# Scores and second mixing as four 64x64 array tiles instead of two 64x128 tiles

## The chip, the cores and the metric

The kernel runs on one core of one Trainium2 chip. The metric is the device time of one execution in microseconds. The time before is the median of nine runs. A profile is one further execution, recorded by the hardware profiler; its durations belong to that execution.

## The reference

Talking-heads attention over 8 batches, 12 heads, 448 positions and a head dimension of 64, followed by a feed-forward network with a squared ReLU:

```python
scores = scale * np.matmul(q, k.transpose(0, 1, 3, 2))        # scale = 1/8
scores = np.einsum('bhij,hg->bgij', scores, w_pre)            # first mixing of heads
attn = np.exp(scores - np.max(scores, axis=-1, keepdims=True))
attn = attn / (np.sum(attn, axis=-1, keepdims=True) + 1e-09)
attn = np.einsum('bhij,hg->bgij', attn, w_post)               # second mixing of heads
out = np.matmul(attn, v)                                      # to x: 3584 x 768
h = np.maximum(x @ w_in, 0.0)                                 # w_in: 768 x 2048
y = (h * h) @ w_out                                           # w_out: 2048 x 768
```

## The kernel before

The work of a batch goes through these stages, each with its line in the profile:

- **Transposes** (`turn_unit`, L162): q and k arrive with positions on the partitions; TensorE turns them, two heads at a time, into `qT` and `kT` with the head dimension on 64 partitions per head. Each matmul uses 112 rows and 64 columns of the array.
- **Scores** (`score_pair`, L295): for one pair of heads and one block of 128 query positions, each head is one matmul. Its 64 contraction rows are the lower or the upper half of the partitions, its stationary side is 128 query positions wide, and its moving side is the 448 key positions. ScalarE copies one head's result to the tile `S`, VectorE the other's (L298). A batch has four blocks, and a block six pairs of heads: 192 pairs in all.
- **Gather** (`gather`, L310): a DMA on SP's queue re-lays ten query positions of all twelve heads, 120 rows by 448, from `S` to `G`.
- **First mixing** (`mix`, L317): one matmul with the stationary `pre` mixes the heads. ScalarE takes the exponential and the row sum (L321), VectorE the reciprocal (L323), and GpSimd (POOL in the profile) scales the row and subtracts 1/448 into one of the tiles `d` (L325). The rows of `d` stand in two groups of 60, at partitions 0 and 64.
- **Second mixing** (`unmix`, L346): it takes two such tiles of `d` at a time. For each tile, each of four residues `r` of the key position and each row group `y`, a matmul has 60 rows and 128 key positions of `d` as the stationary side and 60 columns of `post` as the moving one, so a block has 2 x 4 x 2 = 16 matmuls. The results of `y = 0` and `y = 1` go to two PSUM banks, and VectorE copies each into `at` (L353). There are 180 blocks.
- **Attention times v** (`av_unit`, L181): 112 rows and 64 columns of the array, with ScalarE adding a bias on the way out (L192).
- **The FFN** (`ffn1_unit`, L228, and `ffn2_unit`, L258): full 128x128 matmuls (the last rows of a batch 128x64), with ReLU on ScalarE (L236), the square on GpSimd (L237) and VectorE's copy to the output (L265).

TensorE and GpSimd run in the order in which the program issues their instructions; the other engines are ordered by a scheduler. A loop over steps `ds` mixes two tiles of ten query positions, issues `unmix` for the two of two steps earlier (`LAG = 2`), puts score pairs and gathers ahead by ten tiles (`AHEAD`), and fills the space in between with FFN units of the batch before, by a budget in nanoseconds written into the program. All PSUM banks, eight of them, come from one pool, `psp`.

A matmul in the program becomes two instructions: a weight load of the stationary side (PEld in the profile) and the matmul proper (PE). The tile of the array that it uses follows from its row count, its column count and the partitions at which its operands and its result start.

Of the kernel before, what the change touches and what calls it, by code (L numbers as in the profile page):

```python
# [14 lines left out]
B, H, S, D = 8, 12, 448, 64  # L15
# [5 lines left out]
PR = S // R  # L21
# [4 lines left out]
BLK_START = [0, 120, 240, 320]  # L26
# [3 lines left out]
HR = H * HQ  # L30
# [13 lines left out]
def kernel(  # L44
# [11 lines left out]
    nc = tc.nc  # L56
    P = nc.NUM_PARTITIONS
# [9 lines left out]
    def bank(name, dtype=F32):  # L67
        return psp.tile([P, 512 if dtype == F32 else 1024], dtype, name=name, tag="ps")
# [44 lines left out]
    post = consts.tile([P, H, HQ], BF16, name="post")  # L113
# [4 lines left out]
    post = post[:, :, :].rearrange("p g i -> p (g i)")  # L118
# [19 lines left out]
    qTs, kTs, bvecs, xts, h2ts, ats = {}, {}, {}, {}, {}, {}  # L138
# [149 lines left out]
    def score_pair(b, blk, p):  # L288

        if (b, blk) not in Sb:  # L290
            Sb[(b, blk)] = work.tile([P, H, S], BF16, name="S", tag="S", bufs=2)
        pss = [bank("s_ps") for _ in range(2)]
        for hh in range(2):
            rs = slice(64 * hh, 64 * hh + 64)
            nc.tensor.matmul(pss[hh][:, 0:S], lhsT=qTs[b][rs, p, BLK_START[blk]:BLK_START[blk] + P],  # L295
                             rhs=kTs[b][rs, p, :], start=True, stop=True)
        for hh, copy in enumerate((nc.scalar.copy, nc.vector.tensor_copy)):
            copy(out=Sb[(b, blk)][:, 2 * p + hh, :], in_=pss[hh][:, 0:S])  # L298

# [29 lines left out]
    def place_of(s):  # L329
        b, t = s  # L330
        part = sum(t >= x for x in PARTS[b % 2]) - 1
        if (b, part) not in ats:
            ats[(b, part)] = attn[(3 * b + part) % 2]
        return ats[(b, part)], 2 + IQ * (t - PARTS[b % 2][part])

    def unmix(pair):

        places = [place_of(s) for s in pair]
        us = [bank("at_ps") for _ in range(2)]
        for x, s in enumerate(pair):  # L340
            d = dsb.pop(s)
            for r in range(R):
                for y in range(2):
                    rows = slice(64 * y, 64 * y + HR)
                    c = 4 * HR * x + HR * r
                    nc.tensor.matmul(us[y][:, c:c + HR], lhsT=d[rows, PR * r:PR * r + P], rhs=post[rows, :],  # L346
                                     start=True, stop=True)
        (at, c), (at2, c2) = places
        for y in range(2):
            src = us[y][0:PR, 0:8 * HR].rearrange("p (x m i) -> p m x i", x=2, i=HQ)  # L350
            if at is at2:
                dst = at[0:PR, :, :, c:c + 2 * IQ].rearrange("p r g (x z i) -> p (r g) x z i", z=2, i=HQ)
                nc.vector.tensor_copy(out=dst[:, :, :, y, :], in_=src)  # L353
            else:
                for x, (a, p) in enumerate(places):
                    dst = a[0:PR, :, :, p + HQ * y:p + HQ * y + HQ].rearrange("p r g i -> p (r g) i")
                    nc.vector.tensor_copy(out=dst, in_=src[:, :, x, :])
# [20 lines left out]
    with tc.manual_schedule(engines={PE, POOL}):  # L378
        for x in range(4):
            if x < 3:  # L380
                turn_unit(0, 1, x)
                turn_unit(0, 0, x, nc.scalar.copy)
            if x > 0:
                score_pair(0, 0, 2 * x - 2)
                score_pair(0, 0, 2 * x - 1)
# [26 lines left out]
        def scores_for(ds):  # L412
            tile = 2 * ds + AHEAD + 2
            blk = sum(tile >= x for x in starts) - 1
            if blk + 1 >= len(blocks):
                return
            if blk == 3:
                want = NPAIR * 4 + 2 * max(0, ds - FIRST_TURN[1])
            else:
                into, size = tile - starts[blk] - 2, starts[blk + 1] - starts[blk] - 2  # L420
                want = NPAIR * (blk + 1) + -(-NPAIR * into // size)
            while issued[0] < min(want, NPAIR * (blk + 2)):
                score_pair(*blocks[issued[0] // NPAIR], issued[0] % NPAIR)
                issued[0] += 1
# [12 lines left out]
        for ds in range(nd + LAG):  # L437
# [23 lines left out]
            if old2:  # L461
                unmix(old2)
                for b1, t1 in old2:
                    ends = PARTS[b1 % 2]
                    if t1 + 1 in ends:
                        part = ends.index(t1 + 1) - 1
                        for u in av_units(b1, part):
                            at_step(ds + 1, u)
                        if b1 == 0:
                            c = (IQ * ends[part], min(IQ * ends[part + 1], S))  # L470
                            at_step(ds + 1, (0, lambda c=c: filler.extend(ffn1_units(0, *c))))
                    if t1 == NT - 1:
                        if b1 > 0:
                            at_step(ds + 1, (0, lambda b1=b1: filler.extend(ffn1_units(b1))))
                        at_step(ds + 1, (0, lambda b1=b1: filler.extend(ffn2_units(b1))))
# [38 lines left out]
```

The softmax here doesn't subtract the row's maximum and nothing guards it: scores larger than these inputs give would overflow.

## Time and profile before

| | |
|---|---|
| median of 9 runs | 629.05 us (626.99 to 630.07) |
| profiled execution | 629.31 us, span of its trace 627.5 us |
| TensorE matmuls (PE) | busy 575.4 us, 7,530 instructions |
| TensorE weight loads (PEld) | busy 321.5 us, 7,530 instructions |
| VectorE / ScalarE / GpSimd | busy 423.0 / 396.4 / 409.3 us |
| granted TensorE clock, mean | 0.975 |

The span runs from the first to the last instruction of the trace. Matmuls are pipelined and their ends are modelled, so a matmul's duration is a latency; what it costs is the distance from its start to the next start. A group's row reads: line, engine, operation, output<-input, shapes, count, then busy time and mean duration, then the idle time before it and what ended it. In the TensorE rows "60\*128 60x60" means 60 rows and 128 columns of the array, and a moving operand of 60 partitions by 60 elements.

### The profile page before, as it was taken

The numbers are of one execution on the slowest core, as the hardware profiler recorded it, in microseconds if no ns is written. First come the engines' busy times: TensorE is split into PE (matmuls) and PEld (weight loads), VectorE is DVE, ScalarE is ACT, GpSimd is POOL, SyncE is SP. The second block draws the span as 40 slices with busy tenths as digits, with TensorE's granted clock in tenths as the row PEclk, the third lists the DMA queues.
The fourth block names the chain that finished last, engine by engine and source line by source line (L and its number), as shares of the span: only waits on it lengthen the run. The fifth ranks groups of instructions, "written<-read, shape, count | busy, mean of one in ns | idle before, by whom it ended". The sixth has DMA issues, their size and how long they took to land.

```text
span 627.5 us, 19617 instructions
## 1 busy us (share of the span) xinstructions
PE 575.4 (92%) x7530; PEld 321.5 (51%) x7530; DVE 423.0 (67%) x1082; ACT 396.4 (63%) x1196; POOL 409.3 (65%) x615
## 2 busy tenths in 40 slices
PE   4466898899999999999999999999999999999897
PEld 3123565655545555545645455545545555555554
DVE  3365886888777677866877677767877777654101
ACT  3455676677677757776677647876678657862320
POOL 6374959876388835895388835896387646872450
PEclk9965999999999999999999999999999999999899
DMA  9999969779547965587546964587553755422002
GB/s 139 191 193 186 178 122 151 131 105 171 135 90 115 159 138 106 97 130 112 121 104 112 156 137 101 97 134 120 119 102 75 129 121 102 76 58 76 15 11 78
DMA packets 90882, 73.64 MB, mean 117 GB/s; under 512 B 6308, under 2 KB 87716, under 8 KB 90788
## 3 DMA queue, kind: packets, MB, share of 16 engines
q1 hardware_dynamic: 51842, 49.57, 35.1%
q0 software_dynamic: 38816, 22.81, 28.4%
q8 instruction: 59, 0.97, 0.6%
q14 instruction: 35, 0.29, 0.1%
q10 hardware_dynamic: 130, 0.01, 0.0%
HBM read 45.63 MB, written 11.01 MB: 90 GB/s over the span
## 4 chain that ended last, share of the span: by engine, by line
PE 63%; POOL 10%; DMA 9%; ACT 7%; DVE 5%; issue 2%; SPq 2%; ACTq 0%; DVEq 0%; POOLq 0%
PE o_ps L258 22%; PE h_ps L228 19%; DMA G<-S 8%; PE m_ps L317 8%; PE at_ps L346 6%; POOL d L325 4%; PE s_ps L295 4%; PE ot_ps L181 4%; POOL h L237 3%; ACT xt L192 3%; ACT e_sb L321 3%; PE tr_ps L162 2%; DVE at L353 2%; SPq L310 2%; DVE S L298 1%
## 5 line engine op out<-in xcount | busy, mean ns | idle before, releaser
L325 POOL TENSOR_SCALAR d<-e_sb,rc 128x448 bf16<-128x448 f32 x360 | 225.6, 638 | 164.6 <-DVE rc L323 162.2
L321 ACT ACTIVATE e_sb<-m_ps 128x448 f32<-128x448 f32 x360 | 195.1, 556 | 77.2 <-PE m_ps L317 64.3
L353 DVE CAST at<-at_ps 112x480 bf16<-112x480 f32 x352 | 221.5, 669 | 32.8 <-PE at_ps L346 31.8
L228 PE MATMUL h_ps<-xt,w 128*128 128x448 bf16 (+2 forms) x960 | 168.2, 316 | 2.8 <-ACT e_sb L321 1.4
L258 PE MATMUL o_ps<-w,h 128*128 128x384 bf16 (+1 forms) x1024 | 162.5, 327 | 1.3 <-POOL h L237 1.3
L237 POOL TENSOR_TENSOR h<-hr 128x448 bf16<-128x448 f32 (+2 forms) x160 | 123.7, 780 | 28.8 <-ACT hr L236 26.0
L228 PEld LDWEIGHTS <-w 128*128 128x128 bf16 x960 | 82.6, 98 | 78.0 <-issue 21.0
L258 PEld LDWEIGHTS <-h 128*128 128x128 bf16 (+1 forms) x1024 | 85.3, 100 | 70.0 <-issue 15.5
L298 ACT CAST S<-s_ps 128x448 bf16<-128x448 f32 x192 | 99.8, 549 | 29.9 <-PE s_ps L295 20.1
L298 DVE CAST S<-s_ps 128x448 bf16<-128x448 f32 x192 | 112.5, 607 | 6.3 <-PE s_ps L295 3.2
L317 PE MATMUL m_ps<-G,pre 120*128 120x448 bf16 x360 | 104.9, 366 | 12.9 <-DMA G<-S 9.7
L323 DVE RECIPROCAL rc<-sm 128x1 f32<-128x1 f32 x360 | 54.6, 158 | 92.0 <-ACT e_sb L321 89.7
L236 ACT ACTIVATE hr<-h_ps 128x448 f32<-128x448 f32 (+2 forms) x136 | 68.3, 502 | 46.8 <-PE h_ps L228 31.1
L295 PE MATMUL s_ps<-kT,qT 64*128 64x448 bf16 x384 | 74.2, 373 | 13.6 <-ACT S L298 8.5
L346 PEld LDWEIGHTS <-d 60*128 60x128 bf16 x2880 | 53.7, 94 | 63.7 <-issue 46.9
L346 PE MATMUL at_ps<-post,d 60*128 60x60 bf16 x2880 | 75.0, 190 | 5.1 <-ACT xt L192 1.3
L321 ACT ACTIVATION_READ_ACCUMULATOR e_sb<-m_ps 128x1 f32 x360 | 77.8, 216 | 0.0
L192 ACT ACTIVATE xt<-ot_ps,bvec 128x160 bf16<-128x160 f32 (+3 forms) x144 | 42.5, 391 | 44.9 <-PE ot_ps L181 31.4
L317 PEld LDWEIGHTS <-pre 120*128 120x128 bf16 x360 | 29.2, 98 | 53.2 <-issue 20.9
L265 DVE COPY osb<-o_ps 128x384 f32<-128x384 f32 x48 | 26.5, 553 | 40.0 <-PE o_ps L258 39.1
L181 PE MATMUL ot_ps<-at,v 112*64 112x160 bf16 (+4 forms) x1152 | 44.7, 237 | 3.5 <-DVE at L353 3.5
L181 PEld LDWEIGHTS <-v 112*64 112x64 bf16 x1152 | 41.1, 114 | 7.4 <-issue 6.5
(36 smaller groups left out, 193.5 us busy)
## 6 DMA issues: line engine op xcount, KB each, us to landing
G<-S SPq DMA_DIRECT2D x352, 105.0 KB
kst<-in_k_dram POOLq DMA_DIRECT2D x24, 224.0 KB, 5.9
qst<-in_q_dram POOLq DMA_DIRECT2D x24, 224.0 KB, 5.7
v<-in_v_dram POOLq DMA_DIRECT2D x24, 224.0 KB, 6.6
w<-in_moe_w_in_dram POOLq DMA_DIRECT2D x8, 384.0 KB, 10.5
w<-in_moe_w_out_dram POOLq DMA_DIRECT2D x8, 384.0 KB, 7.7
out_dram<-osb SPq DMA_DIRECT2D x8, 336.0 KB
out_dram<-osb SPq DMA_DIRECT2D x8, 288.0 KB
```

The lines of the kernel that those rows point to most:

```text
L181: nc.tensor.matmul(ps[64 * hh:64 * hh + 64, TW * y + c0:TW * y + 2 + n], lhsT=vs[b][0:PR, g, r, :], rhs=at[0:PR, r, g, c0:2 + n], start=(y ...
L228: nc.tensor.matmul(ps[:, 0:n], lhsT=w1[ft // 4][:, c2, ft % 4 * 128:ft % 4 * 128 + 128], rhs=xts[b][:, c2, c0:c1], start=(c2 == 0), stop=( ...
L236: nc.scalar.activation(out=hr[:, 0:n], in_=ps[:, 0:n], func=ACT.Relu)
L237: nc.gpsimd.tensor_tensor(out=h2ts[(b, ft)][:, c0:c1], in0=hr[:, 0:n], in1=hr[:, 0:n], op=ALU.mult)
L258: nc.tensor.matmul(dst, lhsT=h2ts[(b, ft)][:, mt * 128:mt * 128 + ROWS[mt]], rhs=w2[ft // 4][:, ft % 4, n2 * 384:(n2 + 1) * 384], start=(f ...
L295: nc.tensor.matmul(pss[hh][:, 0:S], lhsT=qTs[b][rs, p, BLK_START[blk]:BLK_START[blk] + P], rhs=kTs[b][rs, p, :], start=True, stop=True)
L298: copy(out=Sb[(b, blk)][:, 2 * p + hh, :], in_=pss[hh][:, 0:S])
L317: nc.tensor.matmul(ps[:, 0:S], lhsT=pre[0:n, :], rhs=Gs.pop(s)[0:n, :], start=True, stop=True)
L321: nc.scalar.activation(out=e[:, :], in_=ps[:, 0:S], func=ACT.Exp, scale=SCALE, accum_out=sm[:, 0:1])
L325: nc.gpsimd.tensor_scalar(out=d[:, 0:S], in0=e[:, :], scalar1=rc[:, 0:1], scalar2=-1.0 / S, op0=ALU.mult, op1=ALU.add)
L346: nc.tensor.matmul(us[y][:, c:c + HR], lhsT=d[rows, PR * r:PR * r + P], rhs=post[rows, :], start=True, stop=True)
L353: nc.vector.tensor_copy(out=dst[:, :, :, y, :], in_=src)
```

## The change

Each score matmul is split into two with 64 query positions each, written to the lower and the upper 64 partitions of the same bank. Each matmul of the second mixing is split the same way, over its 128 key positions. Both therefore use tiles of 64 rows by 64 columns: a pair of heads takes four matmuls instead of two, a block of the second mixing 32 instead of 16. The moving operands (448 and 60 columns), the results in PSUM, the copies and the order of the stages stay as they were. In the second mixing the four tiles of a residue `r` follow one another: `y = 0` lower and upper half, then `y = 1`; in the scores likewise with the head `hh`.

```diff
@@ score_pair
         for hh in range(2):
             rs = slice(64 * hh, 64 * hh + 64)
-            nc.tensor.matmul(pss[hh][:, 0:S], lhsT=qTs[b][rs, p, BLK_START[blk]:BLK_START[blk] + P],
-                             rhs=kTs[b][rs, p, :], start=True, stop=True)
+            for z in (0, 64):
+                q0 = BLK_START[blk] + z
+                nc.tensor.matmul(pss[hh][z:z + 64, 0:S], lhsT=qTs[b][rs, p, q0:q0 + 64],
+                                 rhs=kTs[b][rs, p, :], start=True, stop=True)
@@ unmix
                     rows = slice(64 * y, 64 * y + HR)
                     c = 4 * HR * x + HR * r
-                    nc.tensor.matmul(us[y][:, c:c + HR], lhsT=d[rows, PR * r:PR * r + P], rhs=post[rows, :],
-                                     start=True, stop=True)
+                    for z in (0, 64):
+                        nc.tensor.matmul(us[y][z:z + 64, c:c + HR], lhsT=d[rows, PR * r + z:PR * r + z + 64],
+                                         rhs=post[rows, :], start=True, stop=True)
```

## The prediction

> **What bounds the kernel now.** I read the page's busy table and slices first, then the stage windows, then the groups, then the timeline of TensorE in a settled stretch.
>
> ```profile
> span 627.5 us, 19617 instructions
> PE 575.4 (92%) x7530; PEld 321.5 (51%) x7530; DVE 423.0 (67%) x1082; ACT 396.4 (63%) x1196; POOL 409.3 (65%) x615
> PEclk9965999999999999999999999999999999999899
> DMA  9999969779547965587546964587553755422002
> PE 63%; POOL 10%; DMA 9%; ACT 7%; DVE 5%; issue 2%; SPq 2%; ACTq 0%; DVEq 0%; POOLq 0%
> ```
>
> TensorE is busy for 92% of the span and holds 63% of the chain that ended last; DMA is full only in the first slices. The windows by stage (columns: length, busy time of each engine, clock, DMA share) separate the two:
>
> ```profile
> 30.00:80.00 50.00, 36.63 (x518) 19.89 (x513) 34.27 (x94) 29.72 (x93) 36.36 (x60) 0.74 1.06 185
> 80.00:580.00 500.00, 484.39 (x6571) 271.25 (x6569) 371.14 (x939) 344.31 (x1057) 344.28 (x515) 1.00 0.63 115
> ```
>
> Before 80 us the DMA queues are full and TensorE waits for them at a low clock. From 80 to 580 us TensorE is busy 97% at full clock and no other engine passes 75%. In that stretch nearly every nanosecond added to TensorE's stream is added to the time. The two groups that the change edits are:
>
> ```profile
> L295 PE MATMUL s_ps<-kT,qT 64*128 64x448 bf16 x384 | 74.2, 373 | 13.6 <-ACT S L298 8.5
> L346 PEld LDWEIGHTS <-d 60*128 60x128 bf16 x2880 | 53.7, 94 | 63.7 <-issue 46.9
> L346 PE MATMUL at_ps<-post,d 60*128 60x60 bf16 x2880 | 75.0, 190 | 5.1 <-ACT xt L192 1.3
> ```
>
> "64\*128" and "60\*128" say that both already run as tiles of 64 rows by 128 columns, two at a time. The 190 ns is a latency and not a cost. The cost is read from the timeline of TensorE (start, length, line, count):
>
> ```profile
> 302.11 0.55 PE L317 MATMUL m_ps<-G,pre 120*128 120x448 bf16 x2
> 302.49 1.46 PE L258 MATMUL o_ps<-w,h 128*128 128x384 bf16 x8
> 303.88 0.39 PE L346 MATMUL at_ps<-post,d 60*128 60x60 bf16 x16
> 304.12 0.35 PE L295 MATMUL s_ps<-kT,qT 64*128 64x448 bf16 x2
> 304.40 0.50 PE L258 MATMUL o_ps<-w,h 128*128 128x384 bf16 x2
> ...
> 306.19 0.58 PE L162 MATMUL tr_ps<-ident,kst 112*64 112x112 bf16 x16
> ```
>
> Take a matmul's own latency off a row and divide by its count less one. o_ps: (1.46 - 0.326)/7 = 162 ns for 384 columns, 0.42 ns a column. The sixteen of L346: 0.39 - 0.187 = 0.20 us from first to last start; the single records say 207 ns: a first step of 39, then about 27.5 ns for each two. Sixty columns at 0.42 ns are 25 ns, so a step is the streaming of sixty columns and little else, and both row halves run at once, as do both score halves (304.12 to 304.40 is 280 ns, and 448 columns are 187). The remaining 93 ns of those 280 are a **mode switch**: wherever the tile shape changes, the next matmul starts 88 to 98 ns later than streaming explains (m_ps to o_ps, same shape: 2 ns). I count 406 switches in the trace, some 39 us. L346 to L295 is no switch: L295 starts when the last sixty columns have streamed.
>
> **What the skill says.** TensorEngine Tiling (Array Packing), Key Properties: changing the tiling mode drains TensorE, and different tiles load and multiply in parallel. The trace agrees with both, at the 88 to 98 ns above and with two tiles at a time; no run shows four yet. The same page, Instruction Overhead, says not to take tiling from a dimension that is already small. TensorE: Matmul & The Clock Gate, Weight-path perf modes: the fast weight load needs 128 columns. The trace agrees: when two loads go back to back, the second starts 15 ns after the first at L346 (128 columns) and 29 ns at L162 (64 columns), and the first step of a block is the load plus the stream, 39 = 13 + 25 at L346 and 73 = 27 + 47 at L162. So a half-wide load takes **27 ns where the full-wide one took 13**. That page's span model gives about 4 ns more for each further tile; the trace has 2 to 4 ns between two tiles.
>
> **The change part by part.**
> - *Number of instructions.* L346 goes from 2,880 load-and-multiply pairs to 5,760, L295 from 384 to 768; TensorE has 10,794 pairs instead of 7,530. Order, waits and increments stay: each split pair stands where the single one stood, the second half needs no wait of its own, and no bank is added.
> - *Streaming.* Nothing is saved. A matmul's time goes with its moving columns, 60 and 448, and these don't change; the halved dimension costs no time. Four quarter arrays do in a step what two half arrays did.
> - *Switches.* None goes. Scores and second mixing shared a mode before and share one after; first mixing and the FFN (128x128) and transposes and AV (128x64) stay apart from it. Cost: nothing.
> - *Second mixing, 180 blocks of 16, then 32.* The first step exposes the half-wide load after the switch: 27 + 25 + 2 = 54 ns instead of 39. In the six further steps a tile's next load can start only after its present matmul has (1.5 ns later in the records), so load and swap take about 29 ns, just over the 27.5 of the stream. The fourth tile starts some 7 ns after the first, where the second started 3 after. New span 54 + 6x29 + 7 = 235 ns against 207: **+28 ns**. Ends: +16 if the load stays hidden (steps of 27.5 and 4 ns of skew less 3), +37 if a step is 31.
> - *Scores, 192 pairs of heads.* Mostly behind a mixing block, so the loads are prefetched: load longer by 2, skew by 4, **+6 ns**; ends 0 and +18 (14 of load exposed and 4 of skew).
> - *Others.* VectorE's copy at L353 and the copies at L298 wait for these matmuls and get their banks 6 to 28 ns later. They have 25% of slack and take 0.55 to 0.67 us each. Hidden. Fetching 43% more TensorE instructions is at most +0.3% of DMA (the page's instruction queue: 0.6%); hidden after 80 us, where DMA is at 0.63.
>
> The sum: 162 mixing blocks and 162 score pairs lie between 80 and 580 us. 162 x 28 = 4.5 us and 162 x 6 = 1.0 us make 5.5. The other blocks stand in the DMA-bound beginning (cover: the G loads; if that cover were gone, +0.5 us) but for two in the tail. By the records TensorE waits 32.7 us of those 500 for others; I let a tenth of the sum fall into such waits: **+5.0 us**. The profiled execution took 629.31 us (span 627.5 and 1.8 around it) and would take 634.3; the median, 629.05, is 0.26 lower, so 634.1. Ends of this case: 162 x 16 x 0.8 = +2.1 and 162 x (37 + 18) = +8.9, 631 to 638.
>
> **Rivals.**
> - *Faster: switches into and out of 64x64 are cheaper.* 324 of the switches between 80 and 580 us touch this mode. It decides from 5.0/324 = 15 ns a switch. If one cost half (48 ns), -15.5 + 5.0 gives 618.6. Against: the kinds of switch in the trace (128x128, 64x128, 128x64, either way) all lie within 88 to 98 ns, whichever dimension changes. Chance 0.10.
> - *Supply or loads in series.* Four half-wide loads that go two after two take 54 ns a step: 8 x 27 = about 200 ns a block, +32 us, 661. Likewise if TensorE gets instructions no quicker than the fastest run shown (32 in 207 ns, 6.5 ns each): 64 take 415 ns, +34 us, 663. For: nothing in the trace asks for 64 in 235 ns. Against: L162's two column tiles and L346's two row tiles start their loads 3 to 4 ns apart, and single instructions follow at 1.6 ns. In part (10 to 15 us) as likely as in full. Chance 0.10.
> - *Four tiles don't run at once, only two.* A block +220 ns, a score pair +187: 162 x 0.407 = +66 us, 695. It would mean that the change doesn't do what it says. Against: either direction works by itself. Chance 0.03.
> - *All of it is hidden* by the 32.7 us of waits: 629.5. For: the chain has 8% of G loads. Against: 97% busy. Chance 0.08.
>
> **How the numbers follow.** The main case has 0.69: 634.1, own range 631 to 638. The measurement tells about 0.2% (1.3 us) from no change, so main, supply and two-at-a-time are slower, 0.82; hidden is the same, 0.08; cheaper switches faster, 0.10. The range 628 to 644 takes in the main case, the hidden one and the partial form of the supply case; outside are about 0.10 below and 0.08 above.
>
> **What would show it.** Right: L346's successor at about 0.42 us per x32 row of the timeline (235 + 187), 93 to 98 ns at each switch as now, still 406 of them, other groups unchanged, window 80 to 580 some 1% longer, and load rows of 64 columns near 110 ns. Wrong: a block above 0.5 us (loads, supply or two at a time, told apart by the spacing of starts inside a group of four), switches below 80 ns, or a shorter span.

## The result and the profile after

The changed kernel takes 636.1 us (median of ten runs, 633.76 to 638.19) against 629.14 us for the kernel before in the same comparison: ratio 1.0116, 95% interval 1.0102 to 1.0131, so 6.4 to 8.2 us **slower**, by little over 1%. The prediction was 634.1 us, range 628 to 644.

The page after, its first lines (span; busy time, share and count of each engine; clock; instruction queue) and its groups for the two edited lines:

```profile
span 634.5 us, 26150 instructions
PE 586.4 (92%) x10794; PEld 337.5 (53%) x10794; DVE 422.9 (67%) x1082; ACT 397.6 (63%) x1196; POOL 409.3 (65%) x615
...
PEclk9676998989999999999999999999999999999899
...
q8 instruction: 84, 1.38, 0.9%
...
L349 PEld LDWEIGHTS <-d 60*64 60x64 bf16 x5760 | 64.7, 110 | 67.5 <-issue 50.0
...
L349 PE MATMUL at_ps<-post,d 60*64 60x60 bf16 x5760 | 85.7, 195 | 5.2 <-ACT xt L192 1.8
L297 PE MATMUL s_ps<-kT,qT 64*64 64x448 bf16 x768 | 76.7, 373 | 3.6 <-ACT e_sb L323 1.8
```

The tiles are now 60\*64 and 64\*64, with 3,264 pairs more. VectorE, ScalarE and GpSimd are busy as long as before; only TensorE's side has grown. The load of L349, halved in width, takes longer in its record (110 ns against 94), the first sign of the slower load; in the single records two loads back to back on one tile start 28 ns apart, where before they started 15 apart. Windows by stage (length, busy time of each engine, clock, DMA share):

```profile
30.00:80.00 50.00, 37.10 (x796) 21.88 (x797) 34.90 (x96) 30.52 (x94) 36.11 (x60) 0.83 1.06 189
80.00:580.00 500.00, 488.00 (x9417) 281.21 (x9417) 368.18 (x935) 344.56 (x1055) 344.26 (x515) 0.99 0.63 114
```

TensorE is at least as full as before (97.6% against 96.9%) and gets a little less done in the same 500 us: VectorE's instructions, a rough measure of progress, fall from 939 to 935. The timeline of TensorE at the place that answers to the one shown before (start, length, line, count):

```profile
292.73 0.81 PE L258 MATMUL o_ps<-w,h 128*128 128x384 bf16 x4
293.48 0.44 PE L349 MATMUL at_ps<-post,d 60*64 60x60 bf16 x32
293.75 0.36 PE L297 MATMUL s_ps<-kT,qT 64*64 64x448 bf16 x4
294.05 0.50 PE L258 MATMUL o_ps<-w,h 128*128 128x384 bf16 x2
```

The block of the second mixing has gone from 0.39 to 0.44 us. In the single records 142 of 178 lone blocks have no wait inside and take 252 or 253 ns from first to last start; before, it was 206 to 211, most often 207. Inside such a block the four tiles start at 0, 3, 7 and 10 ns, so they do run at once. The first step takes 52 ns and the others 31.7, where they took 39 and 27.5. A mode switch costs 92 to 98 ns almost everywhere (up to 119 behind a few score pairs), and there are 406 as before.

To see where the time lies I split the time from each matmul's start to the next one's, between the 41st and the 356th first mixing (478.1 us before), into stream, switch and whatever exceeds them as a wait. This stretch holds 157 mixing blocks. Differences to before in us, for the change and for those of the experiments below that keep its order of work (one trace each; "short loads" is the second form):

| | change | scores only | mixing only | halves in turn | short loads | eight tiles |
|---|---|---|---|---|---|---|
| inside mixing blocks | +7.4 | 0.0 | +7.3 | +10.6 | +2.7 | +34.4 |
| inside score pairs | +1.2 | +0.8 | -0.8 | +2.9 | +3.5 | +4.0 |
| between stages, switches included | 0.0 | +13.8 | +12.6 | -0.8 | +0.7 | -1.7 |
| inside other stages | +0.3 | 0.0 | 0.0 | 0.0 | 0.0 | +0.9 |
| waits | -0.7 | -6.9 | -5.7 | -3.5 | -1.2 | +35.4 |
| sum | +8.3 | +7.8 | +13.4 | +9.2 | +5.6 | +73.0 |

The second mixing carries the loss. The lines of the table are good to a microsecond or two: the mixing-only kernel leaves the scores as they were and still shows -0.8 there, and the 124 switches that fall into this stretch in the scores-only kernel are worth 11.4 us at 92 ns each, where the table has 13.8. For the eight tiles it is rougher still: 157 blocks that each take 277 ns longer make 43.5 us, so part of what passes inside the blocks stands under waits. The part of the trace ahead of the 41st took 1.6 us less than before, which no run explains; the scores-only, mixing-only and halves-in-turn kernels took 0.5 to 0.9 us less there, the short loads 0.1 us more.

### The profile page after: what moved, and what is told of

Same layout as the page of the kernel before. It is cut to its first block, busy times and chain, and to the rows that moved or that the text cites. A ratio compares the mean times of both kernels' runs of the same rounds, so it can differ in the third digit from the quotient of the medians.

```text
span 634.5 us, 26150 instructions
## 1 busy us (share of the span) xinstructions
PE 586.4 (92%) x10794; PEld 337.5 (53%) x10794; DVE 422.9 (67%) x1082; ACT 397.6 (63%) x1196; POOL 409.3 (65%) x615
## 3 DMA queue, kind: packets, MB, share of 16 engines
q0 software_dynamic: 38816, 22.81, 28.1%
## 4 chain that ended last, share of the span: by engine, by line
PE 63%; POOL 9%; ACT 4%; DVE 3%; issue 1%; DMA 1%; ACTq 0%; DVEq 0%
PE o_ps L258 23%; PE h_ps L228 15%; PE m_ps L319 8%; PE at_ps L349 6%; PE ot_ps L181 5%; POOL h L237 4%; POOL d L327 4%; PE s_ps L297 3%; ACT e_sb L323 2%; PE tr_ps L162 2%; DVE at L356 1%; POOL kst L74 1%; ACT xt L192 1%; POOL qst L74 1%; DMA out_dram<-osb 1%
## 5 line engine op out<-in xcount | busy, mean ns | idle before, releaser
L228 PE MATMUL h_ps<-xt,w 128*128 128x448 bf16 (+2 forms) x960 | 170.9, 320 | 2.0 <-ACT e_sb L323 0.7
L319 PE MATMUL m_ps<-G,pre 120*128 120x448 bf16 x360 | 103.9, 363 | 21.4 <-DMA G<-S 11.5
L349 PEld LDWEIGHTS <-d 60*64 60x64 bf16 x5760 | 64.7, 110 | 67.5 <-issue 50.0
L349 PE MATMUL at_ps<-post,d 60*64 60x60 bf16 x5760 | 85.7, 195 | 5.2 <-ACT xt L192 1.8
L297 PE MATMUL s_ps<-kT,qT 64*64 64x448 bf16 x768 | 76.7, 373 | 3.6 <-ACT e_sb L323 1.8
## 6 DMA issues: line engine op xcount, KB each, us to landing
w<-in_moe_w_in_dram POOLq DMA_DIRECT2D x8, 384.0 KB, 11.4
```

The lines of the kernel that those rows point to most:

```text
L228: nc.tensor.matmul(ps[:, 0:n], lhsT=w1[ft // 4][:, c2, ft % 4 * 128:ft % 4 * 128 + 128], rhs=xts[b][:, c2, c0:c1], start=(c2 == 0), stop=( ...
L297: nc.tensor.matmul(pss[hh][z:z + 64, 0:S], lhsT=qTs[b][rs, p, q0:q0 + 64], rhs=kTs[b][rs, p, :], start=True, stop=True)
L319: nc.tensor.matmul(ps[:, 0:S], lhsT=pre[0:n, :], rhs=Gs.pop(s)[0:n, :], start=True, stop=True)
L349: nc.tensor.matmul(us[y][z:z + 64, c:c + HR], lhsT=d[rows, PR * r + z:PR * r + z + 64], rhs=post[rows, :], start=True, stop=True)
```

## The experiments

**One half of the change at a time.** Edit: the diff of the scores alone, then that of the second mixing alone.

> Only the scores are split into 64x64 tiles; the second mixing keeps its 64x128 tiles. Where a score pair follows a mixing block (137 places) there is now one more mode switch: 543 switches instead of 406. Theory stream (what counts is TensorE's stream, and a switch costs 95 ns wherever the tile shape changes): the scores alone cost 162 x 0.012 = 1.9 us, the switches 137 x 0.095 = 13 us, less a fifth that falls into waits: 641 us (638 to 644). Rival: a switch between 64x128 and 64x64 is no real switch (the row split stays), L346 to L297 within 5 ns of streaming: 630.5 us. With x for the scores, y for the mixing and s for the extra switches, this run is x + s, the mixing-only run y + s, and the full change x + y.

> Only the second mixing is split; the scores keep 64x128 tiles. 543 switches again. Theory stream: blocks of 32 take 253 ns from first to last start as in the full change (before 207): 162 x 0.046 = 7.5 us, and 13 us of switches, less a fifth: 645.5 us (642 to 649). Rival (a switch from 64x64 to 64x128 costs nothing): 635 us. If the difference to the scores-only run is about 4.5 us, the mixing and not the scores carries what the full change lost.

Measured: scores only 634.34 us, ratio 1.0080 (1.0062 to 1.0098), by the ratio +5.0 us; mixing only 640.85 us, ratio 1.0186 (1.0166 to 1.0205), +11.7 us. The full change is +7.3 us by its ratio. Their timelines, first of the scores-only kernel and then of the mixing-only one:

```profile
292.61 0.39 PE L348 MATMUL at_ps<-post,d 60*128 60x60 bf16 x16
292.94 0.38 PE L297 MATMUL s_ps<-kT,qT 64*64 64x448 bf16 x4
```

```profile
294.73 0.44 PE L347 MATMUL at_ps<-post,d 60*64 60x60 bf16 x32
295.10 0.36 PE L295 MATMUL s_ps<-kT,qT 64*128 64x448 bf16 x2
```

Subtract the latency of about 0.19 us from the mixing row, and its last start is at 292.82 and 294.98; the scores follow 0.12 us later instead of 0.024. So 64x128 to 64x64 is a full switch, 92 ns one way and 98 the other in the records, and the rival (no real switch) falls. But both runs came in below their expectation, 638 to 644 and 642 to 649. If the three parts simply add up, x + s = 5.0, y + s = 11.7 and x + y = 7.3 give the scores x = 0.3 us, the mixing y = 7.0 us and the 137 extra switches s = 4.7 us, each to about 1 us by the three intervals: some 34 ns of the time for each switch of 92 to 98 ns.

The table puts the rest into waits, which fall by 6 to 7 us, but only a part of that fell at the switch itself. In the stretch of the table, 109 of the 124 scores behind a mixing block had no wait before the change (the gap is at most 25 ns). The mean gap grew by 83 of the 93 ns of a switch in the scores-only kernel and by 79 of 99 in the mixing-only one, so 1.3 and 2.5 us of the added switches replaced a wait there. The other waits shrink in many places, 1.6 and 1.8 us of it between the two matmuls of the first mixing; why those shrink stays open. For the change it follows that its two halves belong together, that the mixing costs nearly all of it, and that the scores cost at most about a microsecond.

**Halves in turn.** Edit, in the second mixing:

```diff
-            for r in range(R):
-                for y in range(2):
-                    for z in (0, 64):
+            for z in (0, 64):
+                for r in range(R):
+                    for y in range(2):
                         ...
```

> The full change, but each tile of d runs through all its residues on the lower 64 output partitions first and then on the upper 64, so that only two different tiles follow one another instead of four. Same 32 matmuls, same loads, same 406 switches. Theory (four tiles really run at once, a tile's own step is 31.7 ns): 16 steps instead of 8, a block about 52 + 14 x 31.7 + 3 = 500 ns instead of 253, 162 x 0.247 = 40 us, less a fifth: 668 us (660 to 678). Rival (the engine gets through 32 instructions in 250 ns whatever their tiles, so the order doesn't count): 636 us.

Measured: 638.51 us, ratio 1.0142 (1.0124 to 1.0160). The expected 668 us is far off and the rival's 636 near. The timeline of this kernel:

```profile
293.85 0.46 PE L349 MATMUL at_ps<-post,d 60*64 60x60 bf16 x31
294.12 0.35 PE L297 MATMUL s_ps<-kT,qT 64*64 64x448 bf16 x1
294.13 0.19 PE L349 MATMUL at_ps<-post,d 60*64 60x60 bf16 x1
294.13 0.38 PE L297 MATMUL s_ps<-kT,qT 64*64 64x448 bf16 x3
```

A score matmul has started **before** the last matmul of the mixing, which the program issues first. The order of starts is not that of the program: a matmul whose tile is free overtakes those that wait for another tile. It happens at 120 of the 137 places where scores follow a mixing block. At the other 17 the first score starts 10 to 261 ns after the last matmul of the mixing. The records carry no program order, so that the engine does this and not the compiler is concluded from that pattern: an order fixed beforehand would have held the last mixing matmul back behind the late score there. Inside the block, too, two matmuls start at 27 and 30 ns, when the lower tiles' second loads cannot be through (their step from a cold start takes 52). So the run did not do what it was made for: the four tiles ran side by side all the same, and a block takes 276 ns instead of 253, not 500. It says nothing against concurrency. The order in the program costs about 2 us against the full change, and the two intervals overlap.

**Shorter loads.** This kernel leaves out part of the result. Edit, in the second mixing, with the copies taking 48 partitions and the rest of the attention tile set to a constant, in the first form by VectorE at the start, in the second by GpSimd later:

```diff
-    us[y][z:z + 64, c:c + HR], lhsT=d[rows, PR * r + z:PR * r + z + 64]
+    us[y][z:z + 48, c:c + HR], lhsT=d[rows, PR * r + z:PR * r + z + 48]
```

> The full change, but each stationary side of the second mixing is 48 key positions wide instead of 64: 64 of 112 key positions of the mixed attention are left out (the copy takes 48 partitions; the rest of the attention tile is a constant, set once at the start). The number of instructions, the moving columns, the tiles and the copies stay. Theory load-bound (the step of 31.7 ns is a half-wide load of 27 ns and 5 ns until the next may start): a load of 48 columns takes 20 ns, so the step falls back to the stream's 27.5, the first one to 45, a block from 253 to about 220 ns; 162 x 0.033 x 0.8 = 4.3 us less than the full change: 632 us (630.5 to 633.5). Rival issue-bound (eight instructions a step at 4 ns each): step 31.7, block 250 or more, 635.5 to 636.5 us.

> As the run with stationary sides of 48 key positions (64 of the 112 key positions of the mixed attention are left out, the copies take 48 partitions), but the constant in the attention tiles is set by GpSimd while it waits for the first exponentials, not by VectorE at the start, where it had put off the first scores by 7.7 us. Theory load-bound: blocks of 220 ns as there, mixing 4.7 us less than in the full change between the 41st and the 356th first mixing; the scores lost 1.7 us of it in that run, so 632.5 to 635 us, middle 633.5. Rival (what a block saves is lost again before the scores): 636 us.

Measured: 640.67 us for the first form, ratio 1.0172 (1.0155 to 1.0188), of which 7.7 us is its late start (the first scores at 19.2 us instead of 11.5). The second form: 635.19 us, ratio 1.0099 (1.0079 to 1.0118). Its page and timeline:

```profile
L349 PEld LDWEIGHTS <-d 60*48 60x48 bf16 x5760 | 58.2, 100 | 70.5 <-issue 50.4
```

```profile
296.96 0.41 PE L349 MATMUL at_ps<-post,d 60*48 60x60 bf16 x32
297.20 0.39 PE L297 MATMUL s_ps<-kT,qT 64*64 64x448 bf16 x4
```

The block falls to 220 ns in both forms, its first step to 46 and the others to 27.5 ns: as many instructions, as many columns to stream, only a narrower load. That is the load-bound theory for the block to about a nanosecond, and the issue-bound rival falls.

The total does not follow. 635.19 us lies just outside the expected 632.5 to 635, nearer to the rival's 636 than to the middle of 633.5, and its interval overlaps that of the full change (636.1 us). In the stretch of the table this kernel is 2.7 us shorter than the change: 4.7 us come back inside the blocks, but the scores behind them lose 2.3. Their four matmuls start over 18 ns instead of 10, which makes about 1.0 of the 2.3; the rest is not explained. Ahead of the stretch it takes 1.6 us longer than the change, whose early gain it doesn't share. So the block shows the cause, and the total shows little of it.

**Eight tiles.** Edit: in both places `z` runs over 0, 32, 64 and 96, with 32 columns each.

> The split is driven one step further: scores and second mixing in tiles of 64 rows by 32 columns, eight at a time, 64 matmuls a block and eight a score pair; 406 switches. Theory (a step is the longest of stream, load and the spacing of the tiles): loads of 32 columns take 13 ns and are hidden, eight matmuls 3.4 ns apart take 27 ns, so a step is 27.5 to 30 ns and a block 40 + 6 x 29 + 24 = 238 ns against 253 with four tiles; a score pair starts over 24 ns instead of 10. Mixing 162 x 15 ns = 2.4 us less than the full change, scores 2.3 us more: 636 us (634 to 639). Rival (instructions come no faster than eight in 31.7 ns): 63 ns a step, a block 450 ns, about 665 us.

Measured: 706.86 us, ratio 1.1257 (1.1209 to 1.1305). The timeline:

```profile
316.30 0.68 PE L349 MATMUL at_ps<-post,d 60*32 60x60 bf16 x64
316.91 1.47 PE L258 MATMUL o_ps<-w,h 128*128 128x384 bf16 x8
```

The block takes 0.68 - 0.19 = 0.49 us, nearly twice as long as the change's, and the records show how. The first 32 matmuls start 3 to 4 ns apart, as I had reckoned, but for a gap of 16 ns after the first eight, all within 124 ns. Then nothing starts for 101 ns, and the other 32 follow at 8.4 ns each, with their loads. The pace breaks after 64 instructions. The Trainium skill (TensorE: Matmul & The Clock Gate, the table at its head) gives TensorE a queue of 64 instructions; the trace agrees with the number.

The break also falls where the block goes over to its second tile of `d`, which could be a rival cause. The blocks with a wait inside tell the two apart: there the break moves with the wait. In 19 blocks the last such wait comes early enough to see it, and in 18 of them the break follows 32 pairs later (a wait before the eighth matmul, a break before the fortieth), in one 36. So what counts is how many instructions have gathered. Why nothing at all starts for 101 ns stays open. My expectation had left this out; the rival, instructions that come too slowly, is right in kind but not from the first instruction on.

The change's own block has 32 pairs, exactly 64 instructions, and its four tiles need 31.7/4 = 7.9 ns a pair. It keeps that pace to its end.

**Fewer switches.** Not the split, but what a common mode could have saved, had there been switches to save. Edit, in the loop over steps, on the kernel before (with two more tiles of `d` and `PAIR_FROM` = 20):

```diff
             if old2:
+                held.append(old2)
+            pair_up = ds >= PAIR_FROM and ds + 1 < nd + LAG
+            due = [] if pair_up and ds % 2 == 0 else list(held)
+            if due:
+                held.clear()
+            for old2 in due:
                 unmix(old2)
                 ...
-            scores_for(ds)
+            if not (pair_up and ds % 2 == 0):
+                scores_for(ds)
```

> Not the split, but what a common mode could have bought: the tiles of before (64x128), with two mixing blocks and their score pairs issued together at every second step from the 20th on, and two more tiles of d. 276 mode switches instead of 406; the same matmuls. Theory (a switch is 95 ns of TensorE's stream, and TensorE bounds): 130 x 0.095 = 12.4 us less, of which half to nine tenths arrive, since in the scores-only run half of the added switch time fell into waits: 618 to 623 us, middle 621. Rival (bunched work waits for banks and for d as long as the switches lasted): 627 us or more.

> The paired visits with the 64x64 tiles of the change. Theory (the split costs its longer blocks, 46 ns each, whatever the number of switches): 6 to 8 us above the paired visits with 64x128 tiles. Rival (the split costs at the switches, so fewer switches make it cheaper): 4 us above them or less.

Measured: 655.31 us with 64x128 tiles, ratio 1.0435 (1.0412 to 1.0458), and 667.11 us with 64x64 tiles, ratio 1.0599 (1.0575 to 1.0623). The theory is wrong by 34 us and the rival right. A visit in the timeline of the first (in brackets the idle time before the row and who ended it):

```profile
301.06 0.61 PE L347 MATMUL at_ps<-post,d 60*128 60x60 bf16 x32
301.51 0.56 PE L296 MATMUL s_ps<-kT,qT 64*128 64x448 bf16 x2
302.26 0.36 PE L296 MATMUL s_ps<-kT,qT 64*128 64x448 bf16 x2 [0.18 <-ACT e_sb L322]
302.78 0.60 PE L296 MATMUL s_ps<-kT,qT 64*128 64x448 bf16 x2 [0.16 <-ACT e_sb L322]
303.32 0.50 PE L259 MATMUL o_ps<-w,h 128*128 128x384 bf16 x2
```

Both mixing blocks go through in 0.61 us with one switch in and out. Then three score pairs take from 301.51 to 303.32, 0.6 us each, where a lone pair took 0.28: of the eight banks the mixing blocks take four and each pair two, and ScalarE, named in the brackets, has yet to empty them; a copy of the scores takes 0.55 us there and 0.61 us on VectorE. Counted from start to start, what exceeds the stream before scores rises from 14.7 to 54.0 us between the 41st and the 356th first mixing. That is three times the 12.4 us that 130 switches are worth, and less the switches saved it makes up nearly all of the 28.1 us by which this stretch grew. The interleaving with FFN work, which costs the switches, also gives the copies their time; that this is why the waits grow is argued from the places of the waits, and no run took the bunching away alone.

With the split on top a visit of two blocks takes 549 ns against 427, 61 ns a block instead of 46: it is 128 instructions long, keeps the pace of 7.9 ns a pair up to about the fiftieth of its 64 pairs, and starts the rest more slowly and unevenly, 34 ns before the last. That this is the same shortage of instructions is argued and not shown. The difference of the two kernels, 10 to 12 us, is above the 6 to 8 expected. No version tried beats the kernel before.

## Why the prediction was right, and where it was not

- **Bound and direction: right.** In the stretch of the table TensorE's stream is the time; of 9.0 us added to it, 8.3 arrived and 0.7 fell into waits. I had let a tenth fall there.
- **No switch saved: right.** 406 before and after, at 88 to 98 ns before and 92 to 98 after, up to 119 behind a few score pairs.
- **Streaming not shortened: right.** A step still holds sixty columns.
- **The mixing block: the mis-sized term.** I predicted +28 ns with an upper end of +37, and it is +46. (The upper end was summed wrong: with steps of 31 ns, 54 + 6 x 31 + 7 = 247 is +40. The block lies above that too.) The first step was right (52 ns against 54). The further steps are 31.7 ns and not 29: that the half-wide load of 27 ns would stick out was the right mechanism, shown by the short loads, but some 3 ns more pass in a step beside the load than I took; what they are stays open. Six steps make 16 ns of it. The skew of the last tile is 10 ns and not 7. For 162 blocks that is 2.9 us more than the 4.5 predicted, and nine tenths of it would by themselves put the time at 636.7.
- **The total came closer by luck.** In the stretch of the table the change costs 8.3 us, 3.3 more than the 5.0 that I had for the whole. The trace starts 1.6 us faster than before, for no reason that a run shows, and without that gain the measured time would stand near 637.7 instead of 636.1.
- **Scores: right.** +1.0 us predicted, +1.2 in the trace, 0.3 from the three totals, give or take 1.
- **Copies on VectorE and ScalarE hidden: right.** Their busy times are unchanged, and TensorE's waits did not grow (-0.7 us).
- **Rivals.** Cheaper switches did not occur. The waits did not hide the change: only 0.7 of 9.0 us fell into them. Four tiles do run at once: a group of four starts within 10 ns, every 31.7. Slow supply did not decide here; where pairs start 3 to 4 ns apart, as with eight tiles, it does from 64 instructions on, at 4.2 ns an instruction. I had the price too high, 6.5, and did not know that 64 instructions come free of it.

## What to carry to other kernels

Splitting a matmul across the stationary dimension saved no time here, since the time went with the moving columns: it doubled the number of loads, and a load of 64 columns took 27 ns where one of 128 had taken 13. It could pay where it makes room for other work in the array, or where it removes mode switches; no run here shows either. For the second, compare the tile shapes of neighbours before and after: these two stages shared one mode already. Don't price a switch at its full length without looking at the waits: of 137 added switches about a third of the length reached the time, and taking 130 away by bunching cost far more in waits than it saved.

## What the hardware showed that I had not expected

- Matmuls on different tiles can start out of program order, unlike what the description of the kernel before says of TensorE: with the halves in turn, a matmul of L297 started ahead of one of L349 that the program issues before it. The Trainium skill (TensorE: Matmul & The Clock Gate, Part 3, what overlaps and what doesn't) says that matmuls start and end strictly in program order; this trace shows starts that do not, and the measurement decides.
- Dense streams of small matmuls: in the eight-tile kernel 32 pairs of load and matmul start within 124 ns, then nothing for 101 ns, and the others at 8.4 ns a pair.
- Where a tile takes a new load for each matmul, as in this block, a step is longer than the load and the stream alike. With the same sixty columns (25 ns) to stream, loads of 64 columns (27 ns) make a step of 31.7 ns. Loads of 48 columns make one of 27.5, as the full-wide ones did; they take 20 ns by an estimate, 48/64 of the 27 ns.
